# A fused attention and MLP kernel: scores by half-row matmuls, and pairs of pieces computed in one held run

## The chip, the cores and the metric

The kernel runs on one core of one Trainium2 chip. The metric is the device time of one execution in microseconds (us), given as the median of several executions. A profile is one execution, recorded by the hardware profiler; its own time stands beside its span below.

## The reference

`S` = 448, head size 64, 8 batches of 12 heads, 3584 tokens, model width 768, hidden width 2048, all in float32:

```
scores = q @ k.T / sqrt(64) - log(S)
attn   = 1 / (1 + exp(-scores))
x      = (attn @ v), heads side by side: 3584 x 768
h      = x @ w_in
g      = h where h >= 1;  0 where h <= -1;  (h + 1)**2 / 4 between
out    = g @ w_out
```

## The kernel before

Two heads make a *pair* (48 pairs, six to a batch). A pair's key positions are cut into four *pieces* (three of 128, and a last one of 64, the middle of the code's `mid`). For each piece `scores` puts k times q for both heads into a PSUM tile `psc` (two banks, one for each head; there are two such tiles). `weigh` then has ScalarE take the sigmoid in place, and make of it a high 16-bit part (`ahl`, ScalarE) and a low one (VectorE). `av` multiplies these parts with v into `pav`, the two heads in the two column halves of the array. Pairs 0 to 7 are in float32 throughout. From pair 8 on, q and k are split into a high and a low 16-bit part (`hl`, made by `prep_b`, by GpSimd from pair 17 on); from pair 14 on v and the attention weights too.

A score in 16 bits is the sum of three products: k high with q high, k low with q high, k high with q low. Before, `prep_b` has SyncE copy the high and low halves of k on top of each other into a stacked tile `qk` (eight DMAs for a pair), so that one matmul on all 128 rows of the array sums the first two products (L409); the third is a matmul on 64 rows, and those of the two heads lie in the two row halves of the array (L418). The last piece of a pair from 14 on has a tile `corner` of its own and takes three whole matmuls (L404).

The rest is the MLP. `up` (batches 0 and 1, L719) and `up_blocks` (batches 2 to 7, L685, matmuls of 224 columns) compute h, `bend` makes g of it on ScalarE and VectorE, `down` (L755) computes the output. The attention of batch b+1 is spread over the MLP of batch b: `step(i)` is called at set places between MLP units and issues loads (`load_pair`), maxima (`prep_a`), the split (`prep_b`), the scores of the next pieces and the products of piece i with v. The tile framework's scheduler then sets the order on each engine by dependences and priorities. `raw` is the pool of loaded pairs, two buffers.

Words used below, of TensorE: a matmul that has the array's 128 rows and 128 columns is *whole* (`128*128` in the rows); two *half-row* matmuls (`64*128`) or two *half-column* matmuls (`128*64`) of the two heads can lie side by side in the array, quarters (`64*64`) too. A *slot* is the time of one whole matmul of 448 columns, or of two such neighbours. A *turn* is a place where the next matmul has another of these forms than the one before it.

## Time and profile before

| | |
|---|---|
| median of 3 runs | 1160.12 us (1157.73 to 1162.56) |
| the profiled execution | 1159.12 us, span 1157.4 us, granted clock of TensorE 0.999 |
| busy share of TensorE, VectorE, ScalarE, GpSimd | 98%, 70%, 62%, 25% |

The span is the time from the first to the last instruction of the program in the profile; the execution's own time is 1.7 us longer. From about 364 us on the program goes in cycles of some 137 us, one for a batch: an up stage of about 68 us and a down stage of about 69 us, with the attention of the next batch spread over both.

### The profile page before, as it was taken

Reading aid. Unit: us, or ns where it says so; the run is one execution under the profiler, and the core shown is the slowest. Engines: PE = TensorE matmul, PEld = TensorE weight load, DVE = VectorE, ACT = ScalarE, POOL = GpSimd, SP = SyncE. Lnnn points to the kernel's source line nnn. Section 1 sums busy time; section 2 is a strip of 40 time slices with the busy share of each in tenths; the row PEclk is TensorE's granted clock in tenths of the full one; section 3 lists DMA queues with packets and bytes.
Section 4 is the critical chain, followed back from the end, with each engine's and each line's share of the span. In section 5 each row is a group of like instructions: output and inputs, shape, how many; then the busy total and the mean of one; then the engine's idle time right before and its main releaser. Section 6 shows DMA issues by size and latency. Waiting matters only on the chain.

```text
span 1157.4 us, 20215 instructions
## 1 busy us (share of the span) xinstructions
PE 1135.0 (98%) x7662; PEld 666.1 (58%) x7662; DVE 815.8 (70%) x1730; ACT 722.1 (62%) x1199; POOL 294.4 (25%) x367
## 2 busy tenths in 40 slices
PE   8899999999999999999999999999999999999998
PEld 2234334444446775567745785457854677558954
DVE  6988886879987895468936787367964589646820
ACT  6978888578666784557754786447764576423410
POOL 0000000001542354324523353325344233210000
PEclk9999999999999999999999999999999999999999
DMA  9943443162564654225632465224742165203300
GB/s 366 380 138 135 143 165 97 50 212 105 192 209 144 239 211 127 76 94 205 219 102 65 145 207 203 66 66 147 264 145 76 53 207 200 100 17 123 133 22 27
DMA packets 58112, 170.00 MB, mean 147 GB/s; under 512 B 8608, under 2 KB 39840, under 8 KB 51872
## 3 DMA queue, kind: packets, MB, share of 16 engines
q1 hardware_dynamic: 56288, 159.29, 39.9%
q10 hardware_dynamic: 1728, 9.44, 2.3%
q8 instruction: 60, 0.98, 0.3%
q14 instruction: 36, 0.29, 0.1%
HBM read 126.94 MB, written 23.40 MB: 130 GB/s over the span
## 4 chain that ended last, share of the span: by engine, by line
PE 76%; DMA 8%; DVE 6%; ACT 4%; POOL 3%; issue 1%; SPq 0%; POOLq 0%; DVEq 0%; ACTq 0%
PE po L755 30%; PE ph L685 23%; PE pav L491 8%; PE ph L719 7%; DMA raw<-qkv 4%; PE psc L409 3%; PE psc L418 3%; DMA w_out_sb<-w_in 2%; PE psc L404 1%; DVE ahl L459 1%; ACT psc L450 1%; POOL hl L373 1%; DVE mixa L625 1%; ACT dump L335 1%; POOL raw L371 1%
## 5 line engine op out<-in xcount | busy, mean ns | idle before, releaser
L755 PE MATMUL po<-ghl,w_out_sb 128*128 128x448 f16 x2304 | 446.9, 353 | 1.8 <-ACT ghl L735 1.8
L755 PEld LDWEIGHTS <-w_out_sb 128*128 128x128 f16 x2304 | 221.5, 98 | 217.2 <-issue 17.6
L685 PE MATMUL ph<-w_in_sb 128*128 128x224 f16 x3024 | 307.7, 259 | 1.7 <-DMA w_in_sb<-blocks 1.3
L685 PEld LDWEIGHTS <-w_in_sb 128*128 128x128 f16 x3024 | 282.6, 98 | 31.1 <-issue 27.6
L459 DVE SCALAR_TENSOR_TENSOR ahl<-psc,ahl 128x896 f16<-128x896 f32 (+1 forms) x170 | 153.0, 900 | 98.8 <-ACT ahl L458 96.9
L450 ACT ACTIVATE psc<-psc,nls,sqk 128x896 f32<-128x896 f32 (+1 forms) x136 | 129.8, 971 | 94.0 <-PE psc L418 76.1
L371 POOL TENSOR_SCALAR raw<-raw,qkv_s 128x448 f32<-128x448 f32 (+1 forms) x93 | 70.9, 777 | 443.8 <-DVE qkv_i L135 355.7
L458 ACT ACTIVATE ahl<-psc 128x896 f16<-128x896 f32 (+1 forms) x170 | 127.0, 762 | 30.6 <-DVE ahl L459 29.4
L719 PE MATMUL ph<-xhl,w_in_sb 128*128 128x448 f16 x576 | 112.5, 353 | 0.0
L335 ACT ACTIVATE dump<-raw 128x448 f16<-128x448 f32 (+1 forms) x105 | 61.6, 587 | 72.0 <-DMA raw<-qkv 71.3
L694 DVE TENSOR_TENSOR xhl<-ph,xhl 128x224 f32<-128x224 f32 x240 | 87.7, 383 | 26.0 <-PE ph L685 19.6
L491 PE MATMUL pav<-ahl,v 128*64 128x448 f16 x748 | 98.2, 360 | 0.4 <-DVE ahl L459 0.4
L735 ACT ACTIVATE ghl<-g 128x448 f16<-128x448 f32 x128 | 72.5, 572 | 37.2 <-DVE g L734 36.7
L732 ACT ACTIVATE g<-xhl,hr,ihr 128x448 f32<-128x448 f32 x96 | 68.7, 752 | 41.8 <-DVE xhl L694 40.8
L736 DVE TENSOR_TENSOR ghl<-g,ghl 128x448 f16<-128x448 f32 x128 | 84.2, 664 | 8.2 <-ACT ghl L735 7.7
L733 DVE SCALAR_TENSOR_TENSOR g<-g,rk 128x448 f32<-128x448 f32 x112 | 79.8, 727 | 13.9 <-ACT g L732 13.5
L719 PEld LDWEIGHTS <-w_in_sb 128*128 128x128 f16 x576 | 54.8, 98 | 58.2 <-issue 8.9
L373 POOL TENSOR_TENSOR hl<-raw,hl 128x448 f16<-128x448 f32 x62 | 72.8, 1194 | 0.0
L409 PE MATMUL psc<-qk 128*128 128x448 f16 x252 | 66.4, 354 | 2.8 <-ACT a L447 1.8
L734 DVE SCALAR_TENSOR_TENSOR g<-xhl,ihs,g 128x448 f32<-128x448 f32 x96 | 66.3, 708 | 0.3
L768 DVE TENSOR_SCALAR o<-po,od 128x448 f32<-128x448 f32 x42 | 28.5, 679 | 53.1 <-PE po L755 53.1
L430 POOL COPY w_in_sb<-hl 64x128 f16<-64x128 f16 x68 | 32.4, 476 | 127.3 <-DVE hl L367 125.4
(151 smaller groups left out, 1131.6 us busy)
## 6 DMA issues: line engine op xcount, KB each, us to landing
w_in_sb<-blocks SPq DMA_DIRECT2D x48, 1344.0 KB, 6.6
raw<-qkv SPq DMA_DIRECT2D x34, 704.0 KB, 4.8
qk<-hl SPq DMA_DIRECT2D x320, 56.0 KB, 2.0
w_out_sb<-w_in SPq DMA_DIRECT2D x16, 768.0 KB, 11.1
out_t<-o SPq DMA_DIRECT2D x48, 224.0 KB, 1.9
blocks<-mixs SPq DMA_DIRECT2D x8, 768.0 KB, 3.5
w_out_sb<-w_out ACTq DMA_DIRECT2D x6, 768.0 KB, 4.6
raww<-w_out ACTq DMA_DIRECT2D x6, 768.0 KB, 5.8
```

The lines of the kernel that those rows point to most:

```text
L371: nc.gpsimd.tensor_scalar(out=rt, in0=rt, scalar1=s[:, t : t + 1], scalar2=1.0, op0=ALU.mult, op1=ALU.mult)
L373: nc.gpsimd.tensor_tensor(out=dst[:, 1, :], in0=rt, in1=hi, op=ALU.subtract)
L409: nc.tensor.matmul(out, kq[:, j, 1, w], kq[:, j, 0, :], start=True, stop=False)
L450: nc.scalar.activation(a, a, AF.Sigmoid, bias=nls, scale=sqk)
L458: nc.scalar.activation(hi, x, AF.Copy, scale=ATT)
L459: nc.vector.scalar_tensor_tensor(out=lo, in0=x, scalar=ATT, in1=hi, op0=ALU.mult, op1=ALU.subtract)
L491: nc.tensor.matmul(pav[j * D : (j + 1) * D, :S], *terms[j][t], start=c == 0 and t == 0, stop=mid and t == len(terms[j]) - 1,)
L685: nc.tensor.matmul(out, w[:, wt, wh, c * P : (c + 1) * P], xc[:, xt, c, xh, :], start=j in (0, 2) and c + wh + xh == 0, stop=c == HC - 1 a ...
L694: add = lambda out, q, other: nc.vector.tensor_tensor(out=out, in0=quarter(q), in1=other, op=ALU.add)
L719: nc.tensor.matmul(ph[:, :S], w_in_sb[:, f, wh, c * P : (c + 1) * P], xhl[:, c, xh, :], start=c == 0 and wh + xh == 0, stop=c == NCC - 1 a ...
L736: (nc.gpsimd if f % GPOOL else nc.vector).tensor_tensor(out=ghl[:, f, 1, :], in0=g, in1=hi, op=ALU.subtract)
L755: nc.tensor.matmul(po[:, :S], w_out_sb[:, f, wh, m * P : (m + 1) * P], ghl[:, f, gh, :], start=f == lo and wh + gh == 0, stop=f == hi - 1 ...
```

## The change

- The stacked copies `qk` and their eight DMAs a pair are gone. A score from pair 8 on (but for the last piece from pair 14 on) is six half-row matmuls: the three products, each as two neighbours for the two heads.
- From pair 14 on `step` is in two pieces at a time: the scores of two pieces, then the products with v of the two pieces before them, all linked one behind the other (`chain`), with a raised priority for all but the first (`RUN_PRIO`). The first matmul of the scores, and the first of the products, waits for all parts of the attention weights of the two pieces before (`when_made`).
- `raw` has three buffers; a pair is loaded one pair earlier (`load_pair(p + 4)`), and the maxima of pair p + 3 are taken at the pair's first piece instead of its third.
- The scales of pair p + 2 are worked out behind the scores of a pair's last piece, with raised priority (`find_scales`, `SUM_PRIO`), no longer when the split begins.

```
-        raws[p] = raw_p.tile([P, 2 * S + VW], F32, tag="raw", name="raw")
+        raws[p] = raw_p.tile([P, 2 * S + VW], F32, tag="raw", name="raw", bufs=3)
...
-        qk = stk_p.tile([P, 2, 2, S], F16, tag="qk", name="qk")
-        for j in range(2):
-            src = slice(j * D, (j + 1) * D)
-            for h in range(2):
-                dst = slice(h * D, (h + 1) * D)
-                nc.sync.dma_start(out=qk[dst, j, 0], in_=hl[src, 0, 0, :])
-                nc.sync.dma_start(out=qk[dst, j, 1], in_=hl[src, 1, h, :])
-        ready[p] = qk, v, sqk, inv, hl
+        ready[p] = hl, v, sqk
...
+    def when_made(some):
+        waits = [ins for i in some if i >= NPC * GROUPED for ins in made.get(i, ())]
+        def once(ins):
+            while waits:
+                tc.add_manual_dep(
+                    ins.ins, waits.pop().ins.name,
+                    mybir.DependencyInfo(mybir.DependencyClass.Sync, mybir.DependencyReason.DATA), reason="group",
+                )
+            return ins
+        return once
+    def chain():
+        begun = []
+        def run(issue):
+            if not begun:
+                begun.append(issue())
+                return
+            with tc.high_priority(offset=RUN_PRIO):
+                ins = issue()
+            tc.add_manual_dep(
+                ins.ins, begun[-1].ins.name,
+                mybir.DependencyInfo(mybir.DependencyClass.NoSync, mybir.DependencyReason.DATA), reason="run",
+            )
+            begun.append(ins)
+        return run
+    def scores(todo, run=None):
+        tiles, once = [], when_made([i - 2 for i in todo])
...
-                kq = ready[p][0]
-                for j in range(2):
-                    out = psc[j * D : (j + 1) * D, 0, :S] if mid else psc[:, j, :S]
-                    nc.tensor.matmul(out, kq[:, j, 1, w], kq[:, j, 0, :], start=True, stop=False)
+                hl = ready[p][0]
+                for t, (kh, qh) in enumerate(((0, 0), (1, 0), (0, 1))):
+                    for j in range(2):
+                        rows = slice(j * D, (j + 1) * D)
+                        out = psc[rows, 0, :S] if mid else psc[:, j, :S]
+                        run(lambda: once(nc.tensor.matmul(
+                            out, hl[rows, 1, kh, w], hl[rows, 0, qh, :], start=t == 0, stop=t == 2
+                        )))
...
-                sums[p + 2] = all_sum(maxes[p + 2], 3, psc[:, 1, :])
+                with tc.high_priority(offset=SUM_PRIO):
+                    find_scales(p + 2, psc[:, 1, :])
...
             load_pair(p + 3)
+            if p + 4 > NFULL + NHALF:
+                load_pair(p + 4)
             prep_a(p + 2)
+            if late:
+                prep_a(p + 3)
         if c == 2:
             prep_b(p + 2)
-            if late:
-                prep_a(p + 3)
-        if i < NPC * (NFULL + NHALF):
+        if i < NPC * GROUPED:
             more, some = i + LAG + 1, [i]
...
+        run = chain() if i >= NPC * GROUPED else None
         if more > state["scored"]:
-            scores(range(state["scored"], more))
+            scores(range(state["scored"], more), run)
             state["scored"] = more
-        for k in some:
-            av(k)
+        av(some, run)
```

Counted over TensorE's whole order of instructions (whatever the change leaves alone, the matmuls of the MLP, of pairs 0 to 7 and of `corner`, has the same count in both):

| | before | after |
|---|---|---|
| scores of pairs 8 to 47 but for `corner`: whole slots (with 6 of two half columns) | 246 | 0 |
| the same: slots of half rows or quarters | 136 | 378 |
| products with v in 16 bits (half columns, 748 matmuls): slots | 398 | 374 |
| turns | 511 | 374 |
| of these in one cycle from the third batch on: slots of scores, corner and products | 36 + 20, 18, 70 | 54, 18, 66 |
| turns in such a cycle | 64 | 42 |

748 matmuls are 374 slots where all go in twos; before, 48 of the stretches hold an odd number.

TensorE, in the up stage of a cycle. Names: `ph` is MLP, `psc` a tile of scores, `pav` the product with v. Before, three pieces of one stretch of the order:

```order
L404 MATMUL psc_5459<-hl_4912,w_in_sb_90 128x448
...
L155 MATMUL psc_5459<-mb_5465,one_96 128x3
...
L491 MATMUL pav_5478<-ahl_5343,v_4913 64x448
L685 LDWEIGHTS w_in_sb_90
L685 MATMUL ph_5392<-w_in_sb_90 128x224
...
L409 MATMUL psc_5634<-qk_5314 128x448
...
L409 MATMUL psc_5637<-qk_5314 128x448
...
L418 MATMUL psc_5634<-hl_5303 128x448
...
L418 MATMUL psc_5637<-hl_5303 128x448
```

Of the change, one run in the same stage (six matmuls of each `psc`, six of the first `ahl` and four of the second, with nothing else between them):

```order
L728 MATMUL ph_5188<-w_in_sb_90 128x224
...
L451 MATMUL psc_5273<-hl_4874 128x448
...
L451 MATMUL psc_5280<-hl_4874 128x448
...
L534 MATMUL pav_5174<-ahl_5165,v_4676 64x448
...
L534 MATMUL pav_5174<-ahl_5169,v_4676 64x448
L728 LDWEIGHTS w_in_sb_90
L728 MATMUL ph_5209<-w_in_sb_90 128x224
```

Before, MLP matmuls stand between a product's matmuls, and whole scores stand between half-row ones; of the change, scores and products of four pieces stand together, and all scores are half-row.

ScalarE, around two wide pieces in the up stage (L450 and L488 are the sigmoid, L458 and L496 the high part, L735 and L778 the 16-bit g of `bend`, L500 and L543 the copy of a finished `pav`). Before:

```order
L450 ACTIVATE psc_5919<-psc_5919,nls_87,sqk_5606 128x2x448
L458 ACTIVATE ahl_5930<-psc_5919 128x896
L735 ACTIVATE ghl_94<-g_5745 128x448
L450 ACTIVATE psc_5922<-psc_5922,nls_87,sqk_5606 128x2x448
L732 ACTIVATE g_5861<-xhl_93,hr1_5103,ihr1_5101 128x448
L500 ACTIVATE x32_92<-pav_5775,sqk_5300 128x448
L732 ACTIVATE g_5867<-xhl_93,hr0_5093,ihr0_5091 128x448
L335 ACTIVATE dump_5915,m3_5914<-raw_5751 128x448
L458 ACTIVATE ahl_5934<-psc_5922 128x896
```

Of the change:

```order
L488 ACTIVATE psc_5858<-psc_5858,nls_87,sqk_5431 128x2x448
L778 ACTIVATE ghl_94<-g_5824 128x448
L488 ACTIVATE psc_5865<-psc_5865,nls_87,sqk_5431 128x2x448
L496 ACTIVATE ahl_5873<-psc_5858 128x896
L778 ACTIVATE ghl_94<-g_5830 128x448
L543 ACTIVATE x32_92<-pav_5738,sqk_5161 128x448
L496 ACTIVATE ahl_5877<-psc_5865 128x896
```

The high part of the second piece stands behind two `ghl` copies and one copy of `pav` now, and behind no `g` and no `dump`.

SyncE's queue in the up stage, before:

```order
L381 DMA qk_5314<-hl_5303 64x448
L661 DMA w_in_sb_90<-blocks_95 128x5376
L319 DMA raw_5454<-qkv 128x1408
...
L380 DMA qk_5620<-hl_5609 64x448
L381 DMA qk_5620<-hl_5609 64x448
```

Of the change:

```order
L322 DMA raw_7084<-qkv 128x1408
L704 DMA w_in_sb_90<-blocks_95 128x5376 x2
L322 DMA raw_7378<-qkv 128x1408
L704 DMA w_in_sb_90<-blocks_95 128x5376 x3
L322 DMA raw_7671<-qkv 128x1408
```

The eight copies of each pair no longer stand between the loads.

## Rows read from the trace of the kernel before

**Rows 1.** The cores (span, mean granted clock), and TensorE's busy time from the page.

```profile
core 0: 1157.4 us, clock 0.999
PE 1135.0 (98%) x7662; PEld 666.1 (58%) x7662; DVE 815.8 (70%) x1730; ACT 722.1 (62%) x1199; POOL 294.4 (25%) x367
```

**Rows 2.** What TensorE waited for in the whole span (releaser, us in total, times, longest).

```profile
PE psc L171 <- DVE diag L161: 2.1, 1, 2.1
PE po L755 <- ACT ghl L735: 1.8, 3, 1.1
PE psc L409 <- ACT a L447: 1.8, 3, 1.0
PE psc L409 <- DMA qk<-hl: 0.6, 1, 0.6
PE psc L404 <- POOL v L373: 0.4, 1, 0.4
```

**Rows 3.** The chain that ended last, in order of time (start us, us, what): where the up stage of two cycles begins.

```profile
501.53 6.14 PE ph L685 x63
638.71 6.14 PE ph L685 x63
```

**Rows 4.** TensorE in order of time (start us, us to the end of the last one, line, matmuls in the stretch): long streams, and a stretch with an odd number of products.

```profile
559.76 4.19 PE L685 MATMUL ph<-w_in_sb 128*128 128x224 f16 x42
563.78 0.54 PE L409 MATMUL psc<-qk 128*128 128x448 f16 x2
564.25 0.36 PE L418 MATMUL psc<-hl 64*128 64x448 f16 x2
564.55 0.76 PE L491 MATMUL pav<-ahl,v 128*64 128x448 f16 x5
565.24 1.90 PE L685 MATMUL ph<-w_in_sb 128*128 128x224 f16 x18
...
588.61 0.92 PE L409 MATMUL psc<-qk 128*128 128x448 f16 x4
589.47 0.55 PE L418 MATMUL psc<-hl 64*128 64x448 f16 x4
589.95 1.14 PE L491 MATMUL pav<-ahl,v 128*64 128x448 f16 x10
591.02 8.12 PE L755 MATMUL po<-ghl,w_out_sb 128*128 128x448 f16 x42
```

**Rows 5.** Groups of matmuls over the whole span (count, busy us, mean ns of one from its start to its modelled end, idle before).

```profile
L755 PE MATMUL po<-ghl,w_out_sb 128*128 128x448 f16 x2304 | 446.9, 353 | 1.8 <-ACT ghl L735 1.8
L685 PE MATMUL ph<-w_in_sb 128*128 128x224 f16 x3024 | 307.7, 259 | 1.7 <-DMA w_in_sb<-blocks 1.3 <-DVE xhl L694 0.4
```

**Rows 6.** TensorE in order of time: a sum of maxima between up matmuls, and one half-row matmul between them.

```profile
539.07 0.17 PE L155 MATMUL psc<-mb,one 128*128 128x3 bf16 x1
539.10 2.56 PE L685 MATMUL ph<-w_in_sb 128*128 128x224 f16 x25
...
542.26 1.90 PE L685 MATMUL ph<-w_in_sb 128*128 128x224 f16 x18
544.09 0.36 PE L418 MATMUL psc<-hl 64*128 64x448 f16 x1
544.38 1.04 PE L685 MATMUL ph<-w_in_sb 128*128 128x224 f16 x9
```

**Rows 7.** Weight loads over the whole span (count, busy us, mean ns).

```profile
L409 PEld LDWEIGHTS <-qk 128*128 128x128 f16 x240 | 22.2, 98 | 18.8 <-issue 7.6 <-DMA qk<-hl 1.1 <-DVE qkv_i L135 0.2
L418 PEld LDWEIGHTS <-hl 64*128 64x128 f16 x240 | 11.2, 93 | 40.3 <-issue 36.9 <-POOL raw L371 3.0 <-ACT x L497 0.4
```

**Rows 8.** Two wide pieces in the up stage, engine by engine in order of time: scores on TensorE, sigmoid and high parts on ScalarE, a low part on VectorE.

```profile
525.65 0.73 PE L409 MATMUL psc<-qk 128*128 128x448 f16 x3
...
526.72 2.06 ACT L450 ACTIVATE psc<-psc,nls,sqk 128x896 f32<-128x896 f32 x2
528.70 1.72 ACT L458 ACTIVATE ahl<-psc 128x896 f16<-128x896 f32 x2
...
531.25 1.08 DVE L459 SCALAR_TENSOR_TENSOR ahl<-psc,ahl 128x896 f16<-128x896 f32 x1
```

**Rows 9.** Busy time in most of an up stage (us, then busy us and instructions of TensorE, weight loads, VectorE, ScalarE, GpSimd; clock, DMA share, GB/s); then the mean of the `ghl` copy in the whole span.

```profile
511.50:571.50 60.00, 60.00 (x537) 46.19 (x535) 54.01 (x114) 48.47 (x89) 27.23 (x34) 1.00 0.63 222
...
L735 ACT ACTIVATE ghl<-g 128x448 f16<-128x448 f32 x128 | 72.5, 572 | 37.2 <-DVE g L734 36.7
```

**Rows 10.** The chain ahead of a wait of TensorE for `ghl` (start us, us, what).

```profile
711.29 1.57 POOL v L373
...
713.16 5.50 DMA raw<-qkv
...
718.74 0.68 ACT dump L335 x2
...
722.75 0.51 ACT ghl L735
...
723.30 0.73 PE po L755 x3
```

**Rows 11.** VectorE in order of time ahead of the longest wait of TensorE (the last block of `mix`, and the diagonal that it waits for).

```profile
336.29 2.96 DVE L625 TENSOR_TENSOR mixa<-w_in_sb 128x768 f32<-128x768 f16 x2 [0.76 <-DMA blocks<-mixs]
344.08 0.27 DVE L161 TENSOR_SCALAR diag<-ident,xm 128x128 bf16<-128x128 bf16 x1
```

More of the change, by code (lines that the diff above doesn't have):

```diff
@@ L56 @@
 CORN = 10
+GROUPED = 14
+RUN_PRIO = 600
+SUM_PRIO = 300
 TP = 1
@@ L355, in prep_b @@
         )
+        sums[p] = s, sqk
+    def prep_b(p):
+        if not NFULL <= p < NPAIR or not first_time("split", p):
+            return
+        r, n = raws.pop(p), 2 if p < NFULL + NHALF else 3
+        if p not in sums:
+            find_scales(p)
+        s, sqk = sums.pop(p)
         hl = hls.pop(p, None) or stk_p.tile([P, 2, 2, S], F16, tag="hl", name="hl")
@@ L394, in scores @@
             tiles.append(psc)
+            run = run if run and i >= NPC * GROUPED else chain()
             if p < NFULL:
@@ new lines, in av @@
+    def av(some, run=None):
+        once, run = when_made(some), run or chain()
+        for i in some:
+            p, c = divmod(i, NPC)
+            b, hp = divmod(p, NP)
+            if c == 0:
+                state["pav"] = ps_av.tile([P, 512], F32, tag="pav", name="pav")
+                if hp == 0:
+                    state["xm"] = sml_p.tile([P, NP], F32, tag="xm", name="xm", bufs=2)
+            pav = state["pav"]
+            at = pieces.pop(i)
+            mid = c == NKC
+            v = ready[p][1]
+            split = p >= NFULL + NHALF
+            terms = []
+            for j in range(2):
+                o = slice(j * D, (j + 1) * D)
+                full_v = slice((2 * c + j) * D, (2 * c + j + 1) * D)
+                if p < NFULL and mid:
+                    full_v = slice(2 * c * D, (2 * c + 1) * D)
+                if not split:
+                    r = o if mid else slice(0, P)
+                    terms.append([(v[r, full_v], at[r, 0 if mid else j, :])])
+                elif mid:
+                    terms.append([(v[:, vh, full_v], at[:, 0, j, :]) for vh in range(2)])
+                else:
+                    terms.append([(v[:, vh, full_v], at[:, ah, j, :]) for vh, ah in ((0, 0), (1, 0), (0, 1))])
+            for t in range(len(terms[0])):
+                for j in range(2):
+                    run(lambda: once(nc.tensor.matmul(
+                        pav[j * D : (j + 1) * D, :S], *terms[j][t],
+                        start=c == 0 and t == 0, stop=mid and t == len(terms[j]) - 1,
+                    )))
```

66 lines of the change are left out of this document (15 added, 51 removed).

## The prediction

> **What bounds the kernel now.** I first looked at the cores and the page: one core, TensorE busy 1135.0 of 1157.4 us, at the full clock [rows 1]. Busy time alone does not say that TensorE's work is the bound, since a matmul counts until its modelled end, past the start of the next, so I next took what TensorE waited for: the five largest entries that the change can touch sum to 6.7 us [rows 2]. Then the chain, for the length of a cycle: the up stages of two batches begin at 501.53 and 638.71, 137.18 us apart [rows 3]. So the time is the length of TensorE's own stream, and the question is what a matmul and a turn cost in it.
>
> TensorE in order of time gives both [rows 4]. The stream of 42 down matmuls runs from 591.02 for 8.12 us; the last one is 0.353 long by the groups [rows 5], so they start (8.12 - 0.353) / 41 = 0.1895 us apart. That is a slot. The up stream gives (4.19 - 0.259) / 41 = 0.096. At 588.61 four whole score matmuls begin, and the half-row ones 0.86 later: 0.86 - 4 x 0.1895 = 0.10 too long. Four half-row matmuls (two slots) take 0.48 until the products: 0.10 too long again. Ten products (five slots) take 1.07 until the next whole matmul: 0.12 too long. So a turn costs 0.10 to 0.12, and no wait stands in the profile for it. Five products at 564.55 take 0.69, three slots and a turn: an odd number pays a whole slot for a half one. A lone half-row matmul at 544.09 holds the array for 0.29, a slot and a turn [rows 6].
>
> The count closes. A cycle has 504 up matmuls (48.4 us), 288 down matmuls (54.6), 36 + 20 + 18 + 70 = 144 slots of attention (27.3), six sums of 0.03 from start to start [rows 6] (0.2) and 64 turns (6.4): 136.9, against 137.18 in the trace.
>
> **The change, part by part.**
>
> *Half-row scores.* 246 whole slots and 136 of half rows become 378 of half rows: the three products of two heads are three slots either way, and only what was split badly is gained: 382 - 378 = 4 slots, 0.8 us. This rests on half-row neighbours going at a slot each in a row of six. The trace has at most two in a row, and those fit 0.48 = 2 x 0.1895 + 0.10 [rows 4]. At a closer look that stretch could hide 0.01 us, since 0.48 is rounded. From below I take nothing, from above 0.01 for each of some 290 slots that follow another, 2.9 us. I take 0.01 once a run, 90 runs, 0.8 us lost, as whole and half-column streams show no more than that after the first two.
>
> *Products in twos.* 398 slots become 374: 24 x 0.1895 = 4.5 us.
>
> *Turns.* 511 become 374: 137 fewer. At 0.10 that is 13.7 us; the bounds are 0.095 (13.0) and 0.12 (16.4). I take 0.10, since two of the three kinds show it.
>
> The sum of the stream is -0.8 + 0.8 - 4.5 - 13.7 = -18.2 us. By cycle: 138 instead of 144 slots and 42 instead of 64 turns, 3.3 us of 137; a reader can check this one number in the trace of the change.
>
> *Copies removed.* 320 DMAs and their place in SyncE's queue go. Only one wait of TensorE, 0.6 us, was for them [rows 2]; I count it as gone.
>
> *Inputs sooner.* The wait for `ghl` (1.8 us in all) has a story in the chain [rows 10]: GpSimd's last step on v frees one of two `raw` buffers at 713.1, the load that wanted it takes 5.50 us, ScalarE stands at the `dump` that reads it, and the `ghl` copies behind it come late; the down matmul begins at 723.30. With a third buffer and a load one pair earlier (a pair is about 23 us) the 5.5 us lie before the need: 1.8 us gained, and the 0.4 of GpSimd's v likewise. So 0.6 + 1.8 + 0.4 = 2.8.
>
> *The diagonal.* 2.1 us are lost where the diagonal comes behind the last block of `mix` on VectorE [rows 2, 11]. In the changed order that block stands ahead of the last run's low parts instead of between them. I take half of it, 1.1.
>
> *The wait added.* A held run begins only when the low parts of the two pieces before are written. Behind it in TensorE's queue stands the whole MLP, so each late run stops the bound engine. Before, the two score tiles made nearly the same demand, piece by piece. How much time is there? Two wide pieces in the up stage took from 525.65 to 531.25 + 1.08 = 532.33, 6.7 us [rows 8]. In the changed order two `ghl` copies of 0.572 [rows 9] stand between, so about 7.8. From one run's start to the next there lie six slots of scores, five of products and three turns (2.4 us) and, where it is tight, 65 up matmuls (6.2): 8.6. So 0.8 us to spare in the up stage; in the down stage there are no `g` copies and at least 39 matmuls (7.4 us) between, so 3 us to spare. With VectorE busy 54.01 of 60.00 us in the up stage [rows 9] some of the 0.8 will be used up. From below nothing, from above 0.25 us for each of the 40 runs in up stages, 10 us (rival 1). I take 0.05 for each of 68 runs, 3.4 us.
>
> In all -18.2 - 2.8 - 1.1 + 3.4 = -18.7 us. The profiled execution took 1159.12 us, with 1157.4 of span; the sum goes against that, 1140.4. The median of the runs before is 1.0 above this execution, so the forecast of the median is **1141 us**. Its own range is 1134 to 1147: the turns' upper bound and no new wait give 1141 - 2.7 - 3.4 = 1135, the half-row upper bound and a mean wait twice as long 1141 + 2.1 + 3.4 = 1146.5.
>
> **Rivals.**
>
> 1. *Part of the gain goes into waits at the runs' starts.* VectorE at 90% in the up stage speaks for it; against it, that the same engines did the same work there before and TensorE's waits were small. With 0.25 us for each of 40 runs, 1141 - 3.4 + 10 = 1148; up to 1154.
>
> 2. *Slower: the up stage becomes bound by ScalarE and VectorE.* If the chain of 7.8 us is 1 us or more late at nearly every up-stage run, since the bends stand between the sigmoids and cannot be passed, TensorE waits. It decides at 18.7 / 40 = 0.47 us a run; at 1.8 us past the slack of 0.8, that is 1 us a run, the time is 1141 - 3.4 + 40 = 1178. Against it: the work on both engines is unchanged, and a cycle 3 us shorter raises VectorE's 90% only to about 93%.
>
> 3. *No change: weight loads show.* In long half-row stretches each slot from the third on could pay its own weight load of 0.093 us [rows 7], since no stretch before is longer than two. About 190 slots x 0.093 = 17.7 us, and the time is 1159. Against it: whole matmuls load 0.098 us of weights each [rows 7] and still follow each other at a slot [rows 4], so loads lie under the matmul before; and the second half-row slot does so too.
> The Trainium skill's page "TensorE: Matmul & The Clock Gate", in Part 3 under what overlaps and what doesn't, speaks against this change: it says that weight loads overlap matmuls in flight only where the row group differs. By that rule every half-row slot after the first would pay, about 290 x 0.093 = 27 us, and the time would be 1168; but by that rule whole matmuls could not run at 0.1895 either, and they do, so I give it little.
>
> 4. *Better.* The waits at the runs' starts do not appear, and the whole of the diagonal's wait goes: 1141 - 3.4 - 1.0 = 1136.6, and with turns at 0.12, 1134.
>
> **How the numbers follow.** The forecast with its range (1134 to 1147) gets 0.64, rival 1 (1147 to 1154) 0.20, rival 4 beyond the range's lower end (under 1134) 0.05, rival 3 0.04, rival 2 0.04, and a middle of waits between rivals 1 and 2 that eats nearly everything (1154 to 1166) 0.03. The range 1134 to 1152 holds the forecast and most of rival 1, some 0.8. A measurement of this kernel tells about 0.5% (5.8 us) from no change. Faster by more than that (under 1154.3): 0.64 + 0.20 + 0.05 = 0.89. Same: rival 3 by its own price and the middle, 0.06. Slower: rival 2 and the page's rule, 0.05.
>
> **What would show it.** In the profile of the changed kernel: a cycle of some 133.5 us between the first `ph` matmuls of two batches; within a run the half-row stretch of two wide pieces six slots long, 1.14 to 1.2 us, and 0.10 at each turn; no `qk`; no wait of a `dump` for `raw` in the down stage, and so none of a down matmul for `ghl`. The step most likely wrong is the wait added: it would stand among TensorE's waits as score matmuls (L451) released by VectorE or ScalarE, in the up stage, where a run's first matmul comes late. If half-row stretches take 0.28 a slot, rival 3 is right. If the cycle is 133.5 but the time is above 1147, look ahead of 364 us, where VectorE is full with `mix` and the orders differ most.

## The result, and the profile after

| | before | after |
|---|---|---|
| median, same chip | 1157.73 us (7 runs) | 1167.01 us (7 runs, 1165.22 to 1168.62) |
| ratio after / before | | 1.0065, 95% interval 1.0049 to 1.008 |
| profiled execution, span | 1159.12, 1157.4 us | 1165.22, 1163.5 us |

The change made the kernel slower, by 0.65%; the forecast was 1141 us. The profile after begins, like [rows 1], with the core, the engines' busy time, and the page's shares of the chain that ended last:

```profile
core 0: 1163.5 us, clock 0.991
PE 1125.7 (97%) x7914; PEld 665.6 (57%) x7914; DVE 827.3 (71%) x1730; ACT 723.9 (62%) x1199; POOL 286.4 (25%) x367
PE 54%; DVE 27%; ACT 13%; issue 3%; DMA 3%; SPq 0%; DVEq 0%; ACTq 0%
```

TensorE is busy 9 us less, and the granted clock is no longer full. In the chain VectorE has 27% and ScalarE 13%; a chain that runs through other engines means that TensorE waited for them. What it waited for (releaser, us in total, times, longest):

```profile
PE ph L728 <- DVE xhl L737: 11.5, 9, 2.2
...
PE ph L728 <- ACT xhl L746: 4.1, 3, 2.5
...
PE psc L174 <- DVE diag L164: 3.4, 1, 3.4
PE psc L451 <- DVE ahl L497: 2.3, 1, 2.3
PE ph L762 <- DVE g L777: 1.2, 1, 1.2
```

(The rows left out are of the float32 pairs at the start.) Against [rows 2], the waits for `qk` and v are gone, and those of 16-bit scores for sigmoids are down from 1.8 to 0.3 us. Down matmuls wait 1.8 us in all as before, now for VectorE (`g` and the low part of `ghl`) and no longer for ScalarE. The diagonal's wait has grown from 2.1 to 3.4, and a new one of 15.6 us leads: matmuls of the up stage (L728) that wait until VectorE (L737) or ScalarE (L746) has taken finished parts of h out of PSUM. The cycle, as in [rows 3]:

```profile
367.39 6.06 PE ph L728 x63
505.47 6.06 PE ph L728 x63
643.56 6.06 PE ph L728 x63
```

That is 138.1 us, where it was 137.2 and 133.5 was forecast. The stream itself did what was forecast. TensorE in order of time, as in [rows 4], a run in the up stage:

```profile
511.46 1.31 PE L451 MATMUL psc<-hl 64*128 64x448 f16 x12
512.70 1.14 PE L534 MATMUL pav<-ahl,v 128*64 128x448 f16 x10
513.77 6.21 PE L728 MATMUL ph<-w_in_sb 128*128 128x224 f16 x63
```

Six half-row slots and a turn take 512.70 - 511.46 = 1.24 us (6 x 0.1895 + 0.10), five slots of products and a turn 1.07. No weight load shows. So the rule of the Trainium skill that the prediction weighed ("TensorE: Matmul & The Clock Gate", Part 3, under what overlaps and what doesn't: weight loads overlap matmuls in flight only where the row group differs) doesn't hold here: by it five of the six slots would pay 0.093 us more [rows 7], 0.5 us in all. That its 1168 us lie near the 1167 measured is chance.

Where the time went, then. I took the starts of all matmuls and put every gap between two of them that is more than 0.06 us beyond its price (a slot, 0.096 for an up matmul, 0.10 for a turn, the float32 prices ahead of pair 8) down as a wait, or as lost clock where the granted clock is 0.5. The rest of the span is the stream:

| us | before | after | difference |
|---|---|---|---|
| stream | 1139.1 | 1118.9 | -20.2 |
| waits in the first 60 us | 6.3 | 6.8 | +0.5 |
| waits later | 11.9 | 28.9 | +17.0 |
| lost in stretches at 1.2 GHz | 0 | 8.9 | +8.9 |
| span | 1157.4 | 1163.5 | +6.1 |

The longest wait of this cycle, as the trace shows it; first TensorE, then VectorE over the same stretch (start us, us, what):

```profile
541.61 4.38 PE L728 MATMUL ph<-w_in_sb 128*128 128x224 f16 x44
548.12 5.08 PE L728 MATMUL ph<-w_in_sb 128*128 128x224 f16 x34 [2.14 <-DVE xhl L737]
```

```profile
541.47 0.38 DVE L737 TENSOR_TENSOR xhl<-ph,xhl 128x224 f32<-128x224 f32 x1
541.77 0.61 DVE L779 TENSOR_TENSOR ghl<-g,ghl 128x448 f16<-128x448 f32 x1
542.30 0.68 DVE L777 SCALAR_TENSOR_TENSOR g<-xhl,ihs,g 128x448 f32<-128x448 f32 x1
542.90 0.61 DVE L779 TENSOR_TENSOR ghl<-g,ghl 128x448 f16<-128x448 f32 x1
543.43 0.15 DVE L130 TENSOR_SCALAR qkv_e<-psc 128x3 f32<-128x3 f32 x1
543.50 0.67 DVE L776 SCALAR_TENSOR_TENSOR g<-g,rk 128x448 f32<-128x448 f32 x1
544.09 0.16 DVE L132 TENSOR_SCALAR qkv_e<-qkv_e 128x3 int32<-128x3 int32 x1
544.16 1.08 DVE L497 SCALAR_TENSOR_TENSOR ahl<-psc,ahl 128x896 f16<-128x896 f32 x1
545.16 0.67 DVE L777 SCALAR_TENSOR_TENSOR g<-xhl,ihs,g 128x448 f32<-128x448 f32 x1
...
545.90 0.61 DVE L779 TENSOR_TENSOR ghl<-g,ghl 128x448 f16<-128x448 f32 x1
546.43 0.38 DVE L737 TENSOR_TENSOR xhl<-ph,xhl 128x224 f32<-128x224 f32 x1
...
547.02 0.62 DVE L497 SCALAR_TENSOR_TENSOR ahl<-psc,ahl 64x448 f16<-64x448 f32 x1
547.67 0.39 DVE L737 TENSOR_TENSOR xhl<-ph,xhl 128x224 f32<-128x224 f32 x1
```

The last L737, which ends at 548.06, is the one that releases TensorE at 548.12. VectorE hardly rests ahead of it. Between the first L737 and the last stand three bend operations L779, three of L776 and L777, two low parts of the attention weights, small operations for the scales of coming pairs, and a single other L737: some 6 us in which VectorE takes one part of h out of PSUM, while TensorE has 44 up matmuls (4.4 us) before it needs that place. ScalarE is as full: from 541.5 to 547.7 us VectorE is busy 6.14 us and ScalarE 6.20 of 6.20.

The second of the two TensorE lines shows the clock too: 34 matmuls, the last starting some 4.8 us after the first, where 33 x 0.096 = 3.2 would do. The granted clock by stretch (us, then busy us of TensorE, loads, VectorE, ScalarE, GpSimd, clock, DMA, GB/s):

```profile
549.00:552.40 3.40, 3.40 (x21) 2.80 (x19) 2.17 (x6) 1.14 (x2) 3.40 (x6) 0.51 0.20 38
...
367.39:505.47 138.08, 134.58 (x1059) 87.76 (x1058) 97.06 (x213) 87.09 (x152) 52.10 (x68) 1.00 0.34 122
505.47:643.56 138.09, 135.75 (x1060) 88.79 (x1058) 96.42 (x213) 87.07 (x152) 52.11 (x68) 0.99 0.34 122
```

The first row lies behind the wait of 2.14 us: 1.2 GHz, the lower level. The two cycles below, one without such a stretch and one with, are equally long. So within a cycle the lower clock took only time that TensorE would have waited a little later; the waits set the cycle.

### The profile page after: what moved, and what is told of

Its sections match the earlier page's. It is cut to its first block, busy times and chain, and to the rows that moved or that the text cites. A ratio compares the mean times of both kernels' runs of the same rounds, so it can differ in the third digit from the quotient of the medians.

```text
span 1163.5 us, 20009 instructions
## 1 busy us (share of the span) xinstructions
PE 1125.7 (97%) x7914; PEld 665.6 (57%) x7914; DVE 827.3 (71%) x1730; ACT 723.9 (62%) x1199; POOL 286.4 (25%) x367
## 4 chain that ended last, share of the span: by engine, by line
PE 54%; DVE 27%; ACT 13%; issue 3%; DMA 3%; SPq 0%; DVEq 0%; ACTq 0%
PE po L798 29%; PE ph L728 8%; PE ph L762 7%; DVE ahl L497 6%; PE pav L534 5%; DVE g L776 4%; PE psc L451 4%; DVE g L777 3%; DVE xhl L737 3%; DVE ghl L779 3%; ACT psc L488 3%; ACT dump L338 2%; ACT g L775 2%; DMA blocks<-mixs 2%; ACT ahl L496 1%
## 5 line engine op out<-in xcount | busy, mean ns | idle before, releaser
L728 PE MATMUL ph<-w_in_sb 128*128 128x224 f16 x3024 | 304.0, 261 | 15.9 <-DVE xhl L737 11.5
L728 PEld LDWEIGHTS <-w_in_sb 128*128 128x128 f16 x3024 | 289.8, 99 | 27.8 <-issue 25.5
L497 DVE SCALAR_TENSOR_TENSOR ahl<-psc,ahl 128x896 f16<-128x896 f32 (+1 forms) x170 | 153.1, 900 | 108.9 <-ACT ahl L496 107.1
L488 ACT ACTIVATE psc<-psc,nls,sqk 128x896 f32<-128x896 f32 (+1 forms) x136 | 129.8, 969 | 114.7 <-PE psc L451 112.3
L381 POOL TENSOR_SCALAR raw<-raw,qkv_s 128x448 f32<-128x448 f32 (+1 forms) x93 | 64.8, 711 | 430.6 <-DVE qkv_i L138 334.7
L496 ACT ACTIVATE ahl<-psc 128x896 f16<-128x896 f32 (+1 forms) x170 | 129.7, 764 | 19.5 <-DVE ahl L497 17.3
L778 ACT ACTIVATE ghl<-g 128x448 f16<-128x448 f32 x128 | 73.0, 572 | 59.1 <-DVE g L777 58.7
L737 DVE TENSOR_TENSOR xhl<-ph,xhl 128x224 f32<-128x224 f32 x240 | 87.8, 384 | 24.4 <-PE ph L728 13.6
L779 DVE TENSOR_TENSOR ghl<-g,ghl 128x448 f16<-128x448 f32 x128 | 88.2, 693 | 12.3 <-ACT ghl L778 11.9
L776 DVE SCALAR_TENSOR_TENSOR g<-g,rk 128x448 f32<-128x448 f32 x112 | 87.5, 793 | 10.9 <-ACT g L775 10.5
L451 PE MATMUL psc<-hl 64*128 64x448 f16 x756 | 88.3, 353 | 2.6 <-DVE ahl L497 2.3
L762 PEld LDWEIGHTS <-w_in_sb 128*128 128x128 f16 x576 | 55.0, 98 | 60.2 <-issue 9.3
L534 PE MATMUL pav<-ahl,v 128*64 128x448 f16 x748 | 84.7, 360 | 0.0
L777 DVE SCALAR_TENSOR_TENSOR g<-xhl,ihs,g 128x448 f32<-128x448 f32 x96 | 71.7, 767 | 0.0
L383 POOL TENSOR_TENSOR hl<-raw,hl 128x448 f16<-128x448 f32 x62 | 69.1, 1135 | 0.0
L534 PEld LDWEIGHTS <-v 128*64 128x64 f16 x748 | 36.8, 110 | 43.6 <-issue 25.8
## 6 DMA issues: line engine op xcount, KB each, us to landing
w_out_sb<-w_in SPq DMA_DIRECT2D x16, 768.0 KB, 11.1
```

Source lines behind the costliest of these rows:

```text
L451: run(lambda: once(nc.tensor.matmul(out, hl[rows, 1, kh, w], hl[rows, 0, qh, :], start=t == 0, stop=t == 2)))
L488: nc.scalar.activation(a, a, AF.Sigmoid, bias=nls, scale=sqk)
L496: nc.scalar.activation(hi, x, AF.Copy, scale=ATT)
L497: made.setdefault(i, []).append(nc.vector.scalar_tensor_tensor(out=lo, in0=x, scalar=ATT, in1=hi, op0=ALU.mult, op1=ALU.subtract))
L534: run(lambda: once(nc.tensor.matmul(pav[j * D : (j + 1) * D, :S], *terms[j][t], start=c == 0 and t == 0, stop=mid and t == len(terms[j]) - ...
L728: nc.tensor.matmul(out, w[:, wt, wh, c * P : (c + 1) * P], xc[:, xt, c, xh, :], start=j in (0, 2) and c + wh + xh == 0, stop=c == HC - 1 a ...
```

## The experiments

The ratios are against the kernel before on the same chip. The times are from several chips, on which the kernel before had medians of 1157.7 to 1160.7 us, so a difference of two times can be off by 1 to 3 us. "Old scales" means that a pair's scales are worked out when its split begins, as before the change. The columns: the profiled execution's turns, stream, waits after the first 60 us and clock loss by the method above; then where the up stage of the first cycle begins, and the length of the second cycle. The first 60 us differ by up to 2 us between executions, so differences of 1 or 2 us in "begins" tell nothing.

| run | time, us | ratio (95%) | turns | stream | waits | clock | begins | cycle |
|---|---|---|---|---|---|---|---|---|
| before | | 1 | 515 | 1139.1 | 11.9 | 0 | 363.8 | 137.2 |
| the change | 1167.0 | 1.0065 (1.0049-1.0080) | 375 | 1118.9 | 28.9 | 8.9 | 367.2 | 138.1 |
| e1_halfrow | 1166.5 | 1.0058 (1.0037-1.0078) | 505 | 1140.7 | 15.5 | 4.6 | 374.6 | 137.4 |
| e4_not_held | 1169.2 | 1.0078 (1.0056-1.0100) | 490 | 1138.3 | 20.4 | 1.4 | 371.4 | 138.1 |
| e2_held_old_inputs | 1159.8 | 0.9996 (0.9985-1.0006) | 379 | 1119.6 | 30.3 | 2.7 | 365.6 | 137.0 |
| e5_old_scales | 1158.8 | 0.9987 (0.9973-1.0001) | 379 | 1119.6 | 29.7 | 1.1 | 365.6 | 137.3 |
| e9_no_low_g | 1152.5 | 0.9941 (0.9923-0.9959) | 379 | 1119.6 | 22.2 | 2.6 | 366.1 | 136.3 |
| e10_before_no_low_g | 1158.7 | 0.9993 (0.9980-1.0005) | 515 | 1140.0 | 10.0 | 3.0 | 367.8 | 137.4 |
| e11_no_dump | 1156.9 | 0.9975 (0.9963-0.9987) | 379 | 1120.2 | 27.5 | 1.0 | 364.9 | 137.4 |
| e12_no_low_g_no_dump | 1151.1 | 0.9926 (0.9907-0.9946) | 379 | 1120.2 | 22.2 | 0.6 | 364.1 | 136.4 |
| e13_late_split | 1166.3 | 1.0058 (1.0035-1.0081) | 374 | 1118.9 | 31.9 | 6.3 | 368.5 | 138.0 |
| e18_no_split | 1150.3 | 0.9909 (0.9894-0.9924) | 379 | 1119.3 | 19.9 | 1.5 | 363.2 | 136.1 |
| e19_after_no_split | 1148.3 | 0.9890 (0.9873-0.9906) | 375 | 1118.9 | 16.9 | 2.4 | 363.1 | 135.4 |
| e20_no_split_no_low_g | 1147.9 | 0.9893 (0.9877-0.9910) | 379 | 1119.2 | 18.6 | 1.6 | 363.4 | 135.9 |
| e6_shift | 1163.8 | 1.0034 (1.0017-1.0052) | 379 | 1119.2 | 33.8 | 1.6 | 364.0 | 138.5 |
| e7_after_shift | 1168.9 | 1.0086 (1.0056-1.0115) | 375 | 1119.0 | 36.3 | 8.1 | 370.3 | 139.4 |
| e8_before_shift | 1166.5 | 1.0058 (1.0037-1.0080) | 548 | 1144.1 | 16.2 | 0.7 | 365.3 | 140.0 |
| e16_share_a | **1150.5** | **0.9909 (0.9892-0.9925)** | 379 | 1119.5 | 21.6 | 1.0 | 366.7 | 135.9 |
| e21_before_share_a | 1171.3 | 1.0090 (1.0063-1.0117) | 621 | 1153.2 | 8.4 | 0 | 364.1 | 139.6 |
| e22_after_share_a | 1168.1 | 1.0068 (1.0048-1.0087) | 375 | 1119.7 | 30.4 | 9.9 | 368.9 | 139.1 |

Some expectations give VectorE's share of the up stage as 95, 91 or 83%, or its work there as 65 to 74 us. Those are sums of durations, which count the overlap of neighbouring instructions twice; by the view of stretches VectorE is busy 84% of the up stage in e5, 82% in e18 and 79% in e12.

### The parts of the change

e1_halfrow: the kernel before with half-row scores and no copies, nothing held.

```
-  nc.tensor.matmul(out, kq[:, j, 1, w], kq[:, j, 0, :], start=True, stop=False)
+  nc.tensor.matmul(out, hl[rows, 1, kh, w], hl[rows, 0, qh, :], start=t == 0, stop=t == 2)
```

> The kernel before with one part of the change alone: scores from pair 8 on by half-row matmuls, no stacked copies and no qk DMAs. Inputs, scales and the freedom of the order are as before. By TensorE's order it has 502 turns (511 before) and 3 slots fewer, so by the sum alone about 1 us less than the kernel before. Theory A (the waits come from holding two pieces together) and theory B (they come from the earlier scales and inputs, which move GpSimd's split onto VectorE's bends) both expect no new waits of ph matmuls for VectorE's adds: within 3 us of before. Theory C (half-row stretches are dearer than they look) expects it slower by 5 us or more.

The time is the one of theory C, but not for its reason: the stream differs by 1.6 us, so half rows are about as dear as forecast. Its cycles are like those of before; 10.8 us are lost ahead of the first cycle, where VectorE makes the blocks for the later batches (`mix`). Three waits there sum to 7 us, but before has 6 us of waits there too; half-clock stretches that follow two of the three lose 4.6, and the stream itself is some 5 us longer there (and 3 to 4 shorter behind). Why this order does worse in that stage I have not settled.

e4_not_held: the change without the held runs (`chain` and `when_made` do nothing).

```
-        waits = [ins for i in some if i >= NPC * GROUPED for ins in made.get(i, ())]
+        waits = []
```

> The changed kernel with nothing held: the matmuls of a run are neither linked nor raised in priority, and no group wait is added. Half-row scores, three raw buffers, earlier loads and earlier scales stay. 487 turns (511 before, 374 changed), 4 slots fewer than before. Theory A expects no 2.3 us waits, and 1153 to 1157. Theory B expects the bends on VectorE as long as in the changed kernel (L776 near 790 ns on average) and waits of the up stage to stay: 1158 to 1168.

115 turns and the odd products come back, 19.4 us of stream, but 8.5 us of waits and 7.5 of lost clock go: holding is worth its 20 us of stream and gives most of it back. Theory A's time is missed by 12 us. As theory B expected, VectorE's g operations are long with nothing held: 778 and 864 ns on average, where the change has 793 and 767.

e2_held_old_inputs: the change with loads, maxima and scales when they were before.

```
-            if p + 4 > NFULL + NHALF:
-                load_pair(p + 4)
...
-                    find_scales(p + 2, psc[:, 1, :])
+                early[p + 2] = all_sum(maxes[p + 2], 3, psc[:, 1, :])
```

> The changed kernel with its inputs as before: two raw buffers, loads and maxima at the old places, scales worked out when the split begins. Held runs and half-row scores stay (378 turns, the same slots as the changed kernel). Theory A (holding) expects the 2.3 us waits of the up stage to stay and a time within 3 us of the changed kernel, 1164 to 1170. Theory B (GpSimd's split moved onto the bends by the earlier scales and inputs) expects the waits and the half-clock stretches gone, VectorE's bends as short as before (L733 at 727 ns on average), and about 1143 to 1150.

e5_old_scales: the change with old scales alone (the second part of that edit).

> The changed kernel with only the scales put back: they are worked out when the split begins instead of right behind the last piece's scores. Held runs, half-row scores, three raw buffers and earlier loads stay (378 turns). If it is the earlier scales that move GpSimd's split onto VectorE's bends (theory B, narrow), the bends are short again, the 2.3 us waits go, and the time is 1143 to 1150. Theory A expects 1164 to 1170 as for the changed kernel.

Both are level with before, 7 to 8 us ahead of the change and between what the two theories expected. So earlier loads and maxima bring next to nothing (the two differ by 1 us), and earlier scales cost 8 (9 by the ratios). In e5 the g operations take 746 and 723 ns, against 793 and 767. In e5 TensorE's waits are many and short (40 with 29.7 us) where the change has 25 with 28.9. All that the shorter stream saves, 19.5 us, is handed back: 17.8 as waits, 1.1 at the lower clock.

The earlier inputs alone on the kernel before were not run.

### What makes the waits

e9_no_low_g: e5, with the low part of g left out from the third batch on.

```
+        if b < SB:
             (nc.gpsimd if f % GPOOL else nc.vector).tensor_tensor(out=ghl[:, f, 1, :], in0=g, in1=hi, op=ALU.subtract)
```

> The change with the scales worked out when the split begins; the low part of g is left out from the third batch on (the old values of the tile are read in its place), which takes 96 operations of some 0.7 us from VectorE and 32 from GpSimd in the bends, and nothing from TensorE. Theory 1: VectorE has 8 to 11 us more room in each of the six up stages, and the waits past the start (30 us) fall to 8 to 13: 1158.8 becomes 1136 to 1144. Theory 2: the waits for the low parts of the attention weights stay and only those for the bends go: 1148 to 1154. If the lost time isn't VectorE's at all: 1156 to 1160.

(It says that GpSimd loses operations too; it doesn't, all 96 were VectorE's.) e10_before_no_low_g is the same edit on the kernel before.

> The kernel before without the low part of g from the third batch on (stale values are read in its place): the control of the run that left it out of the change. 16 operations a batch on VectorE go, about 0.66 us each, and nothing on another engine. If the up stage was bound by TensorE's stream before (its waits in the up stages sum to 2 us), the 10 us a cycle that VectorE gets are worth next to nothing: 1154 to 1158. If VectorE bound both kernels alike, it gains the same 6 us as the change did: 1150 to 1153.

This pair carries the verdict on the main question: the same work taken from VectorE is worth 6.3 us to the change with old scales (1158.8 to 1152.5; 5.3 by the ratios) and about nothing to the kernel before. VectorE's lateness bounds the up stage only once TensorE's stream is shorter. But 15 to 23 us were expected of e9, and three waits of 0.8 to 1.0 us a cycle stay, with VectorE busy 52.03 of 71.00 us:

```profile
502.38:573.38 71.00, 68.82 (x674) 55.99 (x673) 52.03 (x117) 54.57 (x100) 28.68 (x40) 1.00 0.46 168
```

So it isn't mean load alone. e11_no_dump takes the maxima of pairs 18 to 46 from ScalarE instead, e12_no_low_g_no_dump both:

```
+            if p > 17:
+                maxes[p] = held["m"][:, :n]
+                return
```

> The change with the scales worked out when the split begins, and without the maxima of pairs 18 to 46 (the maxima of pair 17 stand for all): three passes of 0.57 us on ScalarE go for each pair, some 7 us of ScalarE in each stage, nothing on VectorE or TensorE. VectorE keeps its 95% of the up stage. If ScalarE's queue makes part of the waits (9 waits of up matmuls, 6.7 us, were released by ScalarE's copies of h): 1158.8 becomes 1150 to 1155 and these are gone. If VectorE alone does: 1156 to 1159.

> Both left out, the low part of g and the maxima of pairs 18 to 46: VectorE at about 83% and ScalarE at about 77% of the up stage. Theory: the waits come from queues that are full and in order on both engines; with room on both the cycle comes down from 137.3 to 134 to 135 us, close to the 133.5 of the forecast, and the time to 1140 to 1146. Rival: a held run needs its two sigmoids, two high and two low parts one after the other, some 6.3 us, and TensorE has only 45 up matmuls (4.3 us) and the products to cover them at the tightest places, so the scores' waits for the low parts (7 us) stay however empty the queues are: 1147 to 1151.

Both fell short: 1.8 us for ScalarE alone, 1.4 beyond e9 for both. No score waits for low parts any more in e12's cycles, so the rival named there falls too. Two waits a cycle are left, and the longest shows its cause: TensorE, two pairs of g operations on VectorE, and GpSimd.

```profile
533.92 1.31 PE L734 MATMUL ph<-w_in_sb 128*128 128x224 f16 x12 [1.50 <-DVE xhl L743]
```

```profile
528.38 2.00 DVE L782 SCALAR_TENSOR_TENSOR g<-g,rk 128x448 f32<-128x448 f32 x2 [0.53 <-ACT g L781]
530.31 2.83 DVE L783 SCALAR_TENSOR_TENSOR g<-xhl,ihs,g 128x448 f32<-128x448 f32 x2
533.06 0.80 DVE L743 TENSOR_TENSOR xhl<-ph,xhl 128x224 f32<-128x224 f32 x2
```

```profile
528.93 0.98 POOL L389 TENSOR_SCALAR v<-raw 128x512 f16<-128x512 f32 x1
529.88 2.77 POOL L390 TENSOR_TENSOR hl<-raw,hl 128x448 f16<-128x448 f32 x2
532.62 1.53 POOL L390 TENSOR_TENSOR v<-raw,v 128x512 f16<-128x512 f32 x1
```

Two such operations take 1.27 us where GpSimd rests (as at 539.68 us of the change); here 2.00 and 2.83, as GpSimd splits a pair.

### GpSimd beside the bends

e13_late_split: the change with the split issued one piece later (`c == 3` for `c == 2`).

> The whole change, scales sooner too, but with the split of pair p + 2 issued at a pair's fourth piece instead of its third. TensorE's work is the same. The change with old scales took 8 us less than the whole change; the two differ in when VectorE does the dozen small operations of the scales and in when GpSimd splits. Theory: what costs is GpSimd's split lying beside VectorE's bends, where an operation with two inputs in SBUF takes up to 1.6 us instead of 0.68; with the split later the bends' means fall to 0.70 or less, and the time to 1157 to 1162. Rival: the small operations ahead of the bends and of the low parts cost, wherever the split lies: 1165 to 1170.

Nothing moved: GpSimd's split lies where it lay (the bends' mean is 0.790 us against 0.793), so this run tells nothing between its theories. The next three take the split itself away: pairs 18 to 47 read pair 17's parts.

```
+        if p > 17:
+            ready[p] = *kept["hv"], sqk
+            return
```

e18_no_split is that on e5, e19_after_no_split on the whole change, e20_no_split_no_low_g on e9.

> The change with the scales worked out when the split begins, and without GpSimd's split of pairs 18 to 47 (pair 17's parts are read for all of them); the scales themselves are still worked out on VectorE. GpSimd keeps only the copies into the corner. Theory: GpSimd's passes beside the bends lengthen VectorE's g operations (2.0 and 2.8 us for two of them where TensorE waited longest in the run without low parts and maxima, against 1.3 alone) and so make the waits: the g operations fall to 0.68, VectorE's share of the up stage to 91% or less, the cycle from 137.3 to 134.5 to 136, the time from 1158.8 to 1145 to 1153. Rival: VectorE's load and the order in its queue make the waits, and collisions only pass them around: 1155 to 1158.

> The whole change (scales sooner) without GpSimd's split of pairs 18 to 47. Theory: what the earlier scales cost is GpSimd's split lying beside the bends, so without it this one and the same with old scales are within 3 us of each other, 1146 to 1155. Rival: the small operations of the scales at high priority cost by themselves, and the 8 us between the two stay: 1156 to 1162.

> Old scales, without GpSimd's split of pairs 18 to 47 and without the low part of g from the third batch on: VectorE with no collisions and 10 us less work in each up stage. If VectorE's lateness, by load and by collisions, is the whole of the waits, the cycle comes to 133.7 to 134.5, TensorE's own stream, and the time to 1138 to 1144. If ScalarE's queue or the chain within a run holds too: 1146 to 1151.

Without the split the change runs at 1148.3, 18.7 us faster, e5 at 1150.3, 8.5 faster. The 8 us that the earlier scales cost are gone, and the rival with the small operations falls. Nor is it that the split came late as an input: no wait of TensorE in the change was released by GpSimd. The split was not taken out of the kernel before; its up matmuls wait 0.4 us in all for VectorE [rows 5], and its waits behind the first 60 us, 11.9 us, bound what it could gain. The bends' groups of the change, and of e18:

```profile
L776 DVE SCALAR_TENSOR_TENSOR g<-g,rk 128x448 f32<-128x448 f32 x112 | 87.5, 793 | 10.9 <-ACT g L775 10.5
L777 DVE SCALAR_TENSOR_TENSOR g<-xhl,ihs,g 128x448 f32<-128x448 f32 x96 | 71.7, 767 | 0.0
```

```profile
L782 DVE SCALAR_TENSOR_TENSOR g<-g,rk 128x448 f32<-128x448 f32 x112 | 75.1, 682 | 9.1 <-ACT g L781 8.3
L783 DVE SCALAR_TENSOR_TENSOR g<-xhl,ihs,g 128x448 f32<-128x448 f32 x96 | 63.0, 681 | 0.2
```

e20 shows what doesn't go: with VectorE busy 50.72 of 70.63 us in the up stage and GpSimd 2.85, the cycle is 135.9 us and still holds 2.2 us of waits (0.6 for ScalarE, 0.8 for the low parts, 0.8 for VectorE). Less these it is 133.7, TensorE's own stream. The low part of g is worth 6.3 us with the split and only 2.4 without (e18 to e20): the two reliefs remove largely the same waits. The last 2 us a cycle, and the diagonal's wait of 2.2, I have not traced to one cause.

### Attention moved to the down stage

e6_shift (on e5), e7_after_shift (on the change) and e8_before_shift (on before): shares of the attention of 6 for an up unit and 11 for a down unit.

```
+        if b >= SB:
+            share = [6 if u < 7 * NFC // 2 else 11 for u in range(last)]
```

> The change, with the scales worked out when the split begins, and from the third batch on with the attention spread unevenly: an MLP unit of the up stage takes 6 shares of it and one of the down stage 11, where both took the same. TensorE's work is the same but for three more turns. Theory 1 (VectorE and ScalarE are full in the up stage, where the bends stand, so what TensorE saves there comes back as waits): attention leaves the stage that is full, the waits of the up matmuls for the bends (11 us) and of the scores for the low parts (8 us) go down to under 8 in all, the time falls from 1158.8 to 1140 to 1147, and the half-clock stretches go with the waits. Theory 2 (holding two pieces makes the waits by itself, since a run needs four parts of attention weights made one after the other): the waits move to the down stage with the runs, 20 to 30 us of them stay, 1155 to 1163.

> The whole change (scales sooner, too) with the attention spread 6 to 11 between up and down stage. Theory 1: the waits of the up stage go, 1167 becomes 1143 to 1153, and the scales worked out sooner still cost some us against the same with old scales, as their collisions of GpSimd with VectorE stay. Theory 2: 1163 to 1170. If the collisions alone made the loss, this and the other run with the same shares differ by the 8 us that the earlier scales cost before; if the collisions cost only because VectorE was full, they differ by under 3.

> The kernel before with the same uneven spread, as the control. Its order gets 29 turns and 4 slots more, 3.7 us by 0.10 a turn. Theory 1: its TensorE stream was the bound, its waits past the start are 12 us in all, so there is little to win: 1158 to 1166. If an even spread is just a bad one for any kernel of this form: 1143 to 1152, and then the uneven run of the change shows nothing on the change.

None got faster; before pays 33 more turns. e6 and e7 differ by 5 us, between the 8 and the 3 that were to decide on the earlier scales, so they don't. e6 looked like a refutation, but its first cycle takes 135.2 us and only the later ones 138.5: attention now ends so late in the down stage that the split of the batch's x falls into the next up stage, and VectorE's work there rises from 60.63 us (e5) to 64.85. The test had put back what it took away. e16_share_a mends that on e5:

```
+            share = [7 if u < 7 * NFC // 2 else 14 if u < last - 14 else 4 for u in range(last)]
```

> A kernel that computes everything: the change with old scales and from the third batch on shares of 7 for an MLP unit of the up stage, 14 for one of the down stage, 4 for its last fourteen, so that attention leaves the up stage but the batch's x isn't late (in the run with 6 and 11 the split of x fell into the next up stage, where VectorE's work rose from 65 to 74 us after the first cycle, of 135.2 us). Theory: each cycle is like that first one, 135 to 136.5 us, and the time 1147 to 1155. If attention in the up stage isn't what fills VectorE: 1158 to 1164.

```profile
366.84 6.06 PE ph L729 x63
502.74 6.06 PE ph L729 x63
638.64 6.06 PE ph L729 x63
```

Each cycle takes 135.9 us now, as expected, and this kernel, which leaves nothing out, beats both others: ratio to before 0.9909 (0.9892 to 0.9925). Against e5 the up matmuls' waits for VectorE and ScalarE fall from 11.1 to 5.6 us, those for ScalarE to none. The same shares on before, and on the whole change:

> The kernel before with the shares 7, 14 and 4, as the control. By the order its stream gets 106 turns more (617 instead of 511, 10.6 us by 0.10 each) and 5 slots more (1 us); its waits past the start are 12 us in all, of which the up stages hold some 2. Theory: the shares help only the change, whose up stage VectorE holds up: before comes to 1164 to 1172. If these shares are simply better for this program: 1145 to 1155.

> The whole change, scales sooner too, with the shares 7, 14 and 4. With old scales these shares took 8 us off. Theory: with fewer splits and low parts in the up stage the collisions cost less too, 1150 to 1158 against 1167 for the change; the same with old scales stays ahead by some us, as the splits of the scales worked out sooner still fall beside the bends. Rival: the collisions of the earlier scales stay as they are, 1158 to 1166.

Before with these shares is slower, its stream 14.1 us longer for 106 turns and 5 slots (0.12 a turn), so the gain is not the shares' alone. The whole change with them is no faster than without, outside what either theory expected. There ScalarE releases most: six waits, 10.5 us.

```profile
PE ph L728 <- ACT xhl L746: 10.5, 6, 2.3
PE ph L728 <- DVE xhl L737: 7.0, 6, 2.2
```

Ahead of one of them ScalarE's part of h stands behind two sigmoids, two high parts, two `ghl` and a copy of `pav`, 5.2 us in a row:

```profile
537.44 2.04 ACT L488 ACTIVATE psc<-psc,nls,sqk 128x896 f32<-128x896 f32 x2
539.41 0.91 ACT L496 ACTIVATE ahl<-psc 128x896 f16<-128x896 f32 x1
...
541.19 0.93 ACT L496 ACTIVATE ahl<-psc 128x896 f16<-128x896 f32 x1
...
542.69 0.38 ACT L746 ACTIVATE xhl<-ph 128x224 f32<-128x224 f32 x1
```

Two pieces at a time come to ScalarE as one block, and what TensorE needs next stands behind it. That holding is the cause of it is my reading and not shown: e16 is held too and has no wait of up matmuls for ScalarE.

## Why the prediction was wrong

- **Half rows, products, turns: right.** -18.2 forecast, -20.2 measured (28 slots, 5.3 us, and 140 turns fewer in the trace, so 0.11 a turn). The count of slots and turns was the sound part; e20's cycle less its waits, 133.7, is the cycle forecast (133.5; by the forecast's own sum 137.2 - 3.3 = 133.9).
- **Inputs sooner, copies: right in kind.** The chain of [rows 10] and the wait for `qk` are gone, but the down matmuls wait 1.8 us for VectorE instead, and with old scales earlier loads and maxima are worth 1 us (e2, e5), not 2.2.
- **Earlier scales: not priced at all.** I took them as part of the inputs. They cost 8 us (e5), which are gone when GpSimd's split is taken away (e18, e19).
- **The diagonal: wrong side.** I took half of 2.1 us off; it is 3.4 (0.8 in e5, with old scales). VectorE is late there still, as in [rows 11].
- **The wait added: the step that failed.** It took 0.05 us for each of 68 runs, 3.4 us. Measured were 17 us more of waits, though the waits it removed are in that too, and 8.9 of lost clock, for which the sum had no term (17.8 and 1.1 in e5, with old scales). The mistake was where it looked. I asked when a *run* could begin, and there the sum held for the change: no score waits for a low part in its up stages, only one in the `mix` stage, 2.3 us. (With old scales, in e5, scores do wait for low parts, 7.9 us in 11 waits.) But the same queues also empty PSUM for the up matmuls. While VectorE and ScalarE do two pieces in a block, the h parts stand behind, and TensorE has less than 5 us of up matmuls before it needs the place. The prediction named the engines and the stage, and the wrong waiting instruction.
- **"VectorE at 90% and 3% more" was the wrong test.** In the 20 us up to the beginning of the wait shown above, 526 to 546 us, VectorE is busy 19.87; the mean of a stage hides this, and also that an operation of 0.68 us takes up to 1.6 beside GpSimd. Before, TensorE's longer stream hid VectorE's load (e10: relief is worth nothing there); its up matmuls waited 0.4 us for VectorE [rows 5].
- **Rival 2 is what happened**, at another instruction: waits and lost clock from 367 us on come to 25 us over the 35 runs of the five up stages that have attention, 0.7 a run, above the 0.47 at which it was said to decide; by its own working, with the waits as measured put in, that gives 1141 - 3.4 + 25 = 1163. It had 0.04. Its argument against, "the work on both engines is unchanged", was true of the work and not of its durations and order.
- The last sign promised held in part: the `mix` stage lost too, 5.5 us of waits more than before between 281 and 355 us, where the forecast saw VectorE full.

## What to carry to other kernels

Shortening the stream of the bound engine is worth only what its neighbours' queues can follow: before counting it, list for the tightest stage everything that stands in their in-order queues between two releases of the PSUM buffers that the engine needs, not only the operations that the edit adds a wait for. Check engines' busy time over stretches as long as the buffers last (here 5 us), not over a stage, and take durations beside GpSimd's work, not the mean. Grouping work to save turns makes blocks on the engines behind; spread the rest of the work so that blocks meet slack (here by the shares, e16; with the earlier scales, e22, the same shares gained nothing).

## What the runs showed of the hardware

VectorE operations with both inputs in SBUF lengthen beside GpSimd, those with an input in PSUM don't. Worked out from the instructions of the change: L776, L777 and L779 take 0.679, 0.677 and 0.620 us alone, and 1.056, 0.966 and 0.914 (up to 1.62) where at least 30% of the operation lies beside GpSimd's; the wide low parts (L497, one input in PSUM) take 1.086 and 1.087, the h parts (L737) 0.384 and 0.385. The Trainium skill's "GPSIMD Engine Reference", section 1 (Specifications), says that GpSimd's way to SBUF is shared with VectorE, with contention for VectorE instructions that have two SBUF inputs: the trace agrees, and adds the price.

In the change TensorE ran at 1.2 GHz in five stretches that sum to 20.5 us, the nearest long wait ahead of each 2.3 to 3.6 us by the method above; its up matmuls were 0.187 us apart there instead of 0.096. Before had none but for its last 1.3 us, and in the change two other waits of 2.3 us (at 408 and 684 us) had none behind them. Within a cycle the loss cost nothing (138.08 and 138.09 us above).
